# Joined response runs, inputs in twos, and half 0's transfers on POOL's queue, in a fused SSM and feed-forward kernel

## The chip, the cores and the metric

The kernel runs on one core of one Trainium2 chip. A core has a matrix engine (PE, with its weight loads shown apart as PEld), a vector engine (DVE), an activation engine (ACT), a general engine (POOL) and a sequencer that only issues transfers (SP). They run from in-order queues of their own and wait for each other by semaphores. Transfers (DMA) are issued from the queues of SP, ACT or POOL. Matmul results go to PSUM, from which ACT or DVE must copy them before the buffer can be used again. The metric is the time of one execution on the device, in microseconds; lower is better.

## The reference

With `x` of 2048 positions and 576 channels, `xn = layernorm(x)`, the result is `x + S4(xn) + FFN(xn)`:

```python
# S4: a convolution along the 2048 positions, channel by channel
P = exp(dt * A * l)                       # A complex, 576 x 128 states, l = 0..2047
K = einsum("dn,dnl,dn->dl", C, P, dt * B).real
y = irfft(rfft(pad(u)) * rfft(pad(K)))[:2048] + u * Dskip
# FFN
out = silu(x @ w1) @ w2                   # 576 -> 4608 -> 576
```

All inputs and outputs are float32.

## The kernel before, in words

The kernel weaves two programs into one stream per engine. The main one is `ffn()`, the feed-forward part. It goes over two halves of the positions, nine chunks of 512 hidden features and two blocks of 512 positions. `up` multiplies `xn` with `w1` (tile `ph`, lines 314 to 316, three products of high and low parts for float32 accuracy), ACT applies SiLU (`gf`, line 322) and casts to a high part (`gh`, 323), DVE subtracts for the low part (`gl`, 324). `down` multiplies with `w2` (tile `po`, 128 x 288, line 339), and DVE adds the result to the tile `acc` of the positions (343). When half 0 is done, `down` stores each `acc` to memory (`dr0`, 346) and loads the residual input of half 1 into the freed tile (`load_x`, 168).

The other program is `side()`, the convolution, which yields between its steps. `weave` advances it when `ffn` has come to a mark, given as a share of `ffn`'s steps. It has these stages:

- phase 0 normalises the input, transposes it for `up` (the later half through memory, `dxt`, reloaded and split by `next_xt` and `split_xt` at lines 353 to 368), and stores `xn` to `dxn`.
- `kgen()` makes the responses `K` of 288 x 2 channels, 8 x 2 at a time, in 36 steps. DVE and ACT make tables `S` and `C`. After every second step PE multiplies them into `kp` (line 675; the array split into column strips, 128 x 32), ACT copies `kp` to `kt` (682), and PE takes the first transform step from `kt` into two tiles `z` (690; the array split into two row halves, 64 x 128). ACT copies `z` into `stage` (698), and every fourth step SP stores `stage` to `d1k` (703).
- `spread()` gives the inputs the same first step: it loads a tile `xr` of `dxn` (145), splits it into `sp` (ACT 150, DVE 151), multiplies it into `pu` (155, 156), copies it to `u1` (157) and stores it to `d1u` (158). It yields 32 times, two for each `xr`. All its buffers are single.
- `spectral()` has 32 steps, each loading rows of `d1u` and `d1k` (797), splitting them, multiplying (`pk`, `pu`), taking the complex product, multiplying back (`pb`, 805), copying to `yo` (757) and storing to `d2` (758, on POOL's queue).
- `tail()` loads `ys` from `d2` (814), in which every load needs all 32 stores, and `add_conv` multiplies them into `py` (826; the array split into 64 x 32) and adds them to the outputs. The last loads of `w1r` and `w2r` use memory that `spectral` has released.

The tiles `kp`, `z`, `pu`, `pk`, `pb` and `py` share three PSUM buffers (`pss`), `po` three others (`ps2`), `ph` two (`ps1`). The order of instructions on each engine is not written out by hand: a scheduler with its own estimates of durations places each instruction; `tc.high_priority()` puts some ahead, and `behind(ins)` keeps the following ones behind `ins`. So moving a mark or a step moves what stands between others.

The lines of `side()` that set when the stages run:

```python
marks = (0.13, 0.597, 0.823)      # kgen from, spectral from, spectral to
for n, at in enumerate(kgen()):
    if n > 1:
        next(sp, None)
    yield marks[0] + at * (marks[1] - marks[0])
```

Of the kernel before, what the change touches and what calls it, by code (L numbers as in the profile page):

```python
# [11 lines left out]
F32 = mybir.dt.float32  # L12
# [7 lines left out]
P = 128  # L20
# [23 lines left out]
def kernel(  # L44
# [21 lines left out]
    nc = tc.nc  # L66
# [14 lines left out]
    d1k = dram.tile([32 * P, D], F32, name="d1k")  # L81
    d2 = dram.tile([32 * P, D], F32, name="d2")
    dxt = [dram.tile([D, 512], F32, name=f"dxt{b}") for b in range(2)]
    dxn = dram.tile([P, NJ, D], F32, name="dxn")
    dr0 = dram.tile([8 * P, D], F32, name="dr0")
# [26 lines left out]
    acc = {}  # L112
# [23 lines left out]
    def behind(ins):  # L136
        return tc.issue_after(ins) if ins is not None else nullcontext()

    def spread(up):

        s1 = up.tile([P, 2, P], F32R, name="s1", bufs=1)
        nc.gpsimd.dma_start(s1, cs1)
        for j in range(NJ):
            src = up.tile([P, D], F32, tag="xr", name="xr")
            nc.sync.dma_start(src, dxn[:, j])
            for m in range(2):
                lo, hi = slice(64 * m, 64 * m + 64), slice(64 - 64 * m, 128 - 64 * m)
                u1 = up.tile([P, D], F32, tag="u1", name="u1")
                sp = up.tile([P, D], F32R, tag="sp", name="sp")
                nc.scalar.copy(sp[lo, :], src[lo, :])  # L150
                nc.vector.tensor_sub(sp[hi, :], src[lo, :], sp[lo, :])
                for h in range(2):
                    hs = slice(h * HD, (h + 1) * HD)
                    pu = pss.tile([P, 512], F32, tag="pss", name="pu")
                    nc.tensor.matmul(pu[:, :HD], s1[:, 0, :], sp[:, hs], start=True, stop=False)  # L155
                    nc.tensor.matmul(pu[:, :HD], s1[:, 1, :], sp[:, hs], start=False, stop=True)  # L156
                    nc.scalar.copy(u1[:, hs], pu[:, :HD])
                nc.gpsimd.dma_start(
                    d1u.rearrange("(p m j) d -> m j p d", m=2, j=NJ)[m, j], u1)
                yield j  # L160
# [86 lines left out]
    def ffn():  # L247
# [78 lines left out]
        def down(blk, jj):  # L326
            half, c, b = blk
            j = 8 * half + 4 * b + jj
            js = slice(jj * P, (jj + 1) * P)
            if half == 1 and c == NCH - 1:  # L330
                if jj % 2 == 0:
                    add_conv(j, (acc[j], acc[j + 1]))
            for h in range(2):
                hs = slice(h * HD, (h + 1) * HD)
                po = ps2.tile([P, 512], F32, tag="ps2", name="po")
                n = 0
                for t in range(FT):
                    for g, w in ((0, 0), (0, 1), (1, 0)):
                        pins["pe"] = nc.tensor.matmul(po[:, :HD], G[blk, t][g][:, js], W2[half, c, t][w][:, hs],  # L339
                                                      start=n == 0, stop=n == 3 * FT - 1).ins  # L340
                        n += 1
                with tc.high_priority():
                    nc.vector.tensor_add(acc[j][:, hs], po[:, :HD], acc[j][:, hs])  # L343
            if half == 0 and c == NCH - 1:
                rows = slice(j * P, (j + 1) * P)
                nc.sync.dma_start(dr0[rows, :], acc[j])
                if j % 2:
                    acc[7 + j], acc[8 + j] = load_x(7 + j, accp, "acc", (nc.sync,))

        def next_xt(b):  # L350

# [211 lines left out]
    def kgen():  # L563
        fT, phiT = kf["f"], kf["phi"]
        with tc.tile_pool(name="kg", bufs=1) as kg:
# [53 lines left out]
                return th  # L619

            stage = None
            tabs = []
            nxt = head(0)
            al = powers(0)
            for i in range(NCK):
# [52 lines left out]
                                if begins:  # L678
                                    first = mm.ins
                tabs = []  # L680
                kt = kg.tile([P, 512], F32, tag="kt", name="kt")
                nc.scalar.copy(kt, kp)

                z = [pss.tile([P, 512], F32, tag="pss", name="z") for _ in range(2)]
                first = None
                for eg in range(4):
                    for h in (1, 0):
                        rows = slice(64 * h, 64 * h + 64)
                        with tc.high_priority(), behind(first):
                            mm = nc.tensor.matmul(z[h][:, eg * P:(eg + 1) * P], kt[rows, eg * P:(eg + 1) * P], f1[rows],  # L690
                                                  start=True, stop=True, tile_position=(64 * h, 0))
                        first = first or mm.ins
                r = (i - 1) % NRUN
                if r == 0:
                    stage = kg.tile([P, 64, NRUN * CH], F32, tag="stage", name="stage")
                sv = stage[:, :, r * CH:(r + 2) * CH].rearrange("p k (e h c) -> p h e k c", h=2, c=2)
                for h in range(2):
                    nc.scalar.copy(sv[:, h], z[h].rearrange("p (e k c) -> p e k c", e=4, c=2))
                if r == NRUN - 2:
                    d0 = (i // NRUN) * NRUN * CH  # L700
                    kv = d1k.rearrange("(k n) (g d) -> g n k d", n=64, g=2)
                    for gp_ in range(2):
                        nc.sync.dma_start(kv[gp_, :, :, d0:d0 + NRUN * CH], stage[gp_ * 64:(gp_ + 1) * 64])
                yield (i + 1) / NCK

        nc.gpsimd.dma_start(d1k.rearrange("(k n) d -> n k d", n=P)[0],
# [2 lines left out]
    def spectral():  # L709
        def operands(k):  # L710
            rows = slice(k * P, (k + 1) * P)
            return load_part(d1u[rows, :], "u"), load_part(d1k[rows, :], "k")

        def front(k):
            if k % 2 == 0:
                mm = kl.tile([P, 2, 4, P], F32R, tag="mm", name="mm")
                nc.gpsimd.dma_start(mm, cm23[:, k:k + 2])
                mats.append(mm)
            mk = mats[-1][:, k % 2]
            us, ks = ops.pop(k) if k in ops else (split_of(t, n) for t, n in zip(operands(k), "uk"))  # L720
            ka = kl.tile([P, D], F32, tag="ka", name="ka")
            kb = kl.tile([P, D], F32, tag="kb", name="kb", bufs=1)
            y = kl.tile([P, D], F32, tag="y", name="y", bufs=1)
            y2 = kl.tile([P, D], F32, tag="y2", name="y2", bufs=1)
            for h in range(2):
                hs = slice(h * HD, (h + 1) * HD)
                pk = pss.tile([P, 512], F32, tag="pss", name="pk")
                mm3(pk[:, :HD], [(mk[:, 0], mk[:, 1], ks)], hs)
                nc.scalar.copy(ka[:64, hs], pk[:64, :HD])
                nc.scalar.copy(ka[64:, hs], pk[:64, :HD])  # L730
                nc.scalar.mul(kb[:64, hs], pk[64:, :HD], -1.0)
                nc.scalar.copy(kb[64:, hs], pk[64:, :HD])
                pu = pss.tile([P, 512], F32, tag="pss", name="pu2")
                mm3(pu[:, :HD], [(mk[:, 0], mk[:, 1], us)], hs)
                nc.vector.tensor_mul(y[:, hs], pu[:, :HD], ka[:, hs])
                nc.vector.tensor_mul(y2[:64, hs], pu[64:, :HD], kb[:64, hs])
                nc.vector.tensor_mul(y2[64:, hs], pu[:64, :HD], kb[64:, hs])
            nc.vector.tensor_add(y, y, y2)
            return mk, split_of(y, "y")

        mats = []
        first = operands(0)
        yield 1.1
        with behind(pins["gh"]):
            ops = {0: [split_of(t, n) for t, n in zip(first, "uk")]}
        yield 1.12
        nxt = front(0)
        for k in range(32):
            mk, ys = nxt
            if k < 31:  # L750
                nxt = front(k + 1)
            yo = kl.tile([P, D], F32, tag="yo", name="yo")
            for h in range(2):
                hs = slice(h * HD, (h + 1) * HD)
                pb = pss.tile([P, 512], F32, tag="pss", name="pb")
                mm3(pb[:, :HD], [(mk[:, 2], mk[:, 3], ys)], hs)
                nc.scalar.copy(yo[:, hs], pb[:, :HD])
            nc.gpsimd.dma_start(d2.rearrange("(p k) d -> k p d", k=32)[k], yo)
            yield 1 + (k + 1) / 32
# [81 lines left out]

    def side():
        nonlocal s4, kl, yp, pa, tail_at
        marks = (0.13, 0.597, 0.823)
        tail_at = (0.91, 0.934, 0.967, 0.0072)
        with tc.tile_pool(name="kf", bufs=1) as kfp:
            for n in ("f", "phi"):
# [49 lines left out]
            with tc.tile_pool(name="up", bufs=1) as up:  # L897
                sp = spread(up)
                for n, at in enumerate(kgen()):
                    if n > 1:  # L900
                        next(sp, None)
                    yield marks[0] + at * (marks[1] - marks[0])
                for _ in sp:
                    pass
# [97 lines left out]
```

## Time and profile before

| | |
|---|---|
| time of the runs | 1112.2 us, median of 3 (1112.11 to 1112.43) |
| profiled execution | 1112.55 us; span of its instructions 1110.8 us |
| PE busy | 1103.5 us, 99% of the span |
| DVE busy | 917.3 us, 83% |
| ACT busy | 708.0 us, 64% |
| POOL busy | 70.8 us, 6% |
| granted PE clock | 0.999 |

A row of the timeline has the start and the duration in us, the engine, the line of the kernel, the operation, the tiles (written <- read), their sizes and how many records it joins; in brackets the idle time of the engine ahead of it and what ended that. Matmuls overlap, so the distance from one start to the next is their pitch, and the duration is longer than it. A float32 matmul of kp or z shows as two records. A view of one tile or of a window gives the smallest, median and largest duration and the same of the time to a transfer's landing. The view of waits names who waited for whom, the total, how often, and the longest.

### The profile page before, as it was taken

Reading aid. Unit: us, or ns where it says so; the run is one execution under the profiler, and the core shown is the slowest. Engines: PE = TensorE matmul, PEld = TensorE weight load, DVE = VectorE, ACT = ScalarE, POOL = GpSimd, SP = SyncE. Lnnn points to the kernel's source line nnn. Section 1 sums busy time; section 2 is a strip of 40 time slices with the busy share of each in tenths; the row PEclk is TensorE's granted clock in tenths of the full one; section 3 lists DMA queues with packets and bytes.
Section 4 is the critical chain, followed back from the end, with each engine's and each line's share of the span. In section 5 each row is a group of like instructions: output and inputs, shape, how many; then the busy total and the mean of one; then the engine's idle time right before and its main releaser. Section 6 shows DMA issues by size and latency. Waiting matters only on the chain.

```text
span 1110.8 us, 22919 instructions
## 1 busy us (share of the span) xinstructions
PE 1103.5 (99%) x9167; PEld 998.1 (90%) x9167; DVE 917.3 (83%) x1546; ACT 708.0 (64%) x1227; POOL 70.8 (6%) x127
## 2 busy tenths in 40 slices
PE   9999999999999999999999999999999999999998
PEld 6888999899889899899989989999999999999887
DVE  7799899999999999999999837787778778784433
ACT  4574456676777676677866536877777778774210
POOL 1101000000000000011000000000000000000111
PEclk9999999999999999999999999999999999999999
DMA  9745521425242515255834163554544445434973
GB/s 255 204 123 152 140 69 61 120 65 128 82 107 81 133 61 131 76 158 155 217 124 105 44 177 102 168 158 129 161 143 151 140 147 169 131 107 129 255 207 86
DMA packets 175851, 148.56 MB, mean 134 GB/s; under 512 B 111088, under 2 KB 142720, under 8 KB 175616
## 3 DMA queue, kind: packets, MB, share of 16 engines
q1 hardware_dynamic: 165408, 112.69, 38.0%
q0 software_dynamic: 9504, 33.49, 9.4%
q8 instruction: 72, 1.18, 0.5%
q10 hardware_dynamic: 832, 0.92, 0.3%
q14 instruction: 35, 0.29, 0.1%
HBM read 102.53 MB, written 44.61 MB: 132 GB/s over the span
## 4 chain that ended last, share of the span: by engine, by line
PE 94%; DMA 2%; DVE 1%; ACT 1%; SPq 1%; issue 0%; POOL 0%; DVEq 0%; ACTq 0%
PE po L339 40%; PE ph L314 34%; PE kp L675 3%; PE ph L315 3%; PE ph L316 3%; PE pu L805 2%; PE pb L805 2%; PE pk L805 2%; PE z L690 2%; PE pu L155 1%; PE py L826 1%; PE pu L156 1%; DMA acc<-in_A_u_dram 1%; DMA dxn<-xj 1%; DMA w1r<-in_B_w_dram 0%; DMA xj<-in_A_u_dram 0%
## 5 line engine op out<-in xcount | busy, mean ns | idle before, releaser
L339 PE MATMUL po<-w2l,gh 128*128 128x288 f32 x1152 | 339.3, 296 | 0.0
L339 PE MATMUL po<-w2h,gl 128*128 128x288 f32 x1152 | 336.9, 295 | 0.0
L339 PE MATMUL po<-w2h,gh 128*128 128x288 f32 x1152 | 336.1, 296 | 0.0
L339 PEld LDWEIGHTS po<-w2h,gh 128*128 128x128 f32 x1152 | 215.3, 188 | 7.5 <-issue 2.8
L339 PEld LDWEIGHTS po<-w2l,gh 128*128 128x128 f32 x1152 | 216.2, 188 | 5.1 <-issue 0.5
L339 PEld LDWEIGHTS po<-w2h,gl 128*128 128x128 f32 x1152 | 215.7, 188 | 0.8
L322 ACT ACTIVATE gf<-ph 128x512 f32<-128x512 f32 (+1 forms) x148 | 86.3, 584 | 142.8 <-PE ph L316 133.6
L314 PE MATMUL ph<-xh,w1h 128*128 128x512 f32 (+1 forms) x592 | 161.8, 388 | 0.7 <-ACT xh L125 0.6
L314 PE MATMUL ph<-xl,w1h 128*128 128x512 f32 (+1 forms) x592 | 161.7, 386 | 0.2 <-DVE xl L126 0.2
L314 PE MATMUL ph<-xh,w1l 128*128 128x512 f32 (+1 forms) x592 | 161.2, 386 | 0.6 <-DVE w1l L283 0.6
L343 DVE TENSOR_TENSOR acc<-po,acc 128x288 f32<-128x288 f32 x288 | 126.4, 451 | 37.8 <-PE po L339 36.3
L324 DVE TENSOR_TENSOR gl<-gf,gh 128x512 fp32r<-128x512 f32 (+1 forms) x148 | 99.0, 672 | 64.3 <-ACT gh L323 63.5
L314 PEld LDWEIGHTS ph<-xh,w1l 128*128 128x128 f32 x592 | 108.1, 188 | 20.9 <-DVE w1l L283 1.1
L314 PEld LDWEIGHTS ph<-xl,w1h 128*128 128x128 f32 x592 | 108.1, 188 | 20.5 <-DVE xl L126 0.7
L314 PEld LDWEIGHTS ph<-xh,w1h 128*128 128x128 f32 x592 | 104.5, 188 | 17.8 <-ACT xh L125 1.2
L323 ACT CAST gh<-gf 128x512 fp32r<-128x512 f32 (+1 forms) x148 | 89.5, 608 | 10.1 <-PE po L339 7.2
L632 ACT ACTIVATE c<-th,magic 128x1040 f32<-128x1040 f32 x36 | 42.1, 1169 | 37.8 <-DVE C L655 27.9
L634 ACT ACTIVATE c<-th 128x1040 f32<-128x1040 f32 x36 | 38.7, 1075 | 33.9 <-DVE th L633 33.8
L300 ACT CAST w2h<-w2r 128x576 fp32r<-128x576 f32 x72 | 47.0, 671 | 17.3 <-PE po L339 14.9
L283 DVE TENSOR_TENSOR w1l<-w1r,w1h 128x640 fp32r<-128x640 f32 x72 | 57.0, 817 | 0.2
L316 PE MATMUL ph<-x,w1l 128*128 128x512 f32 (+1 forms) x148 | 57.0, 386 | 0.0
L315 PE MATMUL ph<-x,w1h 128*128 128x512 f32 (+1 forms) x148 | 57.0, 385 | 0.0
(182 smaller groups left out, 1830.4 us busy)
## 6 DMA issues: line engine op xcount, KB each, us to landing
w2r<-in_B_w_dram SPq DMA_DIRECT2D x72, 288.0 KB, 3.9
w1r<-in_B_w_dram SPq DMA_DIRECT2D x35, 512.0 KB, 3.7
d1u<-u POOLq DMA_DIRECT2D x32, 288.0 KB, 2.4
d1k<-stage SPq DMA_DIRECT2D x18, 512.0 KB, 6.9
ur<-d1u SPq DMA_DIRECT2D x32, 288.0 KB, 3.9
kr<-d1k SPq DMA_DIRECT2D x32, 288.0 KB, 2.7
d<-yo POOLq DMA_DIRECT2D x32, 288.0 KB, 3.2
ys<-d SPq DMA_DIRECT2D x32, 288.0 KB, 11.3
```

The source lines that it names most:

```text
L283: pins["w1l"] = nc.vector.tensor_sub(l1, src, h1).ins
L300: pins["w2h"] = nc.scalar.copy(h2, r2).ins
L314: nc.tensor.matmul(ph, w[:, kt, :], v[:, kt, a:e], start=n + kt == 0, stop=False)
L315: nc.tensor.matmul(ph, h1[:, 4, :], x4[:, a:e], start=False, stop=False)
L316: pins["pe"] = nc.tensor.matmul(ph, l1[:, 4, :], x4[:, a:e], start=False, stop=True).ins
L322: nc.scalar.activation(gf, ph, AF.Silu)
L323: pins["gh"] = nc.scalar.copy(gh, gf).ins
L324: pins["gl"] = nc.vector.tensor_sub(gl, gf, gh).ins
L339: pins["pe"] = nc.tensor.matmul(po[:, :HD], G[blk, t][g][:, js], W2[half, c, t][w][:, hs], start=n == 0, stop=n == 3 * FT - 1).ins
L343: nc.vector.tensor_add(acc[j][:, hs], po[:, :HD], acc[j][:, hs])
L632: nc.scalar.activation(c65, th, AF.Identity, bias=magic)
L805: nc.tensor.matmul(dst, st, mv[:, hs], start=n == 0, stop=n == 3 * len(terms) - 1)
```

## The change

- In `kgen`, a pair's `z` is no longer issued after its own `kp`, but in the new function `along` after the `kp` of the next pair, behind its last matmul. `kt` gets a second buffer. The last pair's `z` follows its own `kt` as before.
- `spread` is advanced twice after every second step of `kgen`, rather than once after each.
- The load of `xr`, half 0's stores to `dr0` and the residual loads go to POOL's queue rather than SP's.
- The responses' last mark goes from 0.597 to 0.615 of `ffn`'s steps. The first two steps of `spectral` go from 1.1 and 1.12 to 1.06 and 1.08 of its own stretch.

```diff
@@ spread
-            nc.sync.dma_start(src, dxn[:, j])
+            nc.gpsimd.dma_start(src, dxn[:, j])
@@ down
-                nc.sync.dma_start(dr0[rows, :], acc[j])
+                nc.gpsimd.dma_start(dr0[rows, :], acc[j])
                 if j % 2:
-                    acc[7 + j], acc[8 + j] = load_x(7 + j, accp, "acc", (nc.sync,))
+                    acc[7 + j], acc[8 + j] = load_x(7 + j, accp, "acc", (nc.gpsimd,))
@@ kgen
+            kts = []
+            def along(first):
+                nonlocal stage
+                i, kt = kts.pop(0)
+                z = [pss.tile([P, 512], F32, tag="pss", name="z") for _ in range(2)]
+                for eg in range(4):
+                    for h in (1, 0):
+                        rows = slice(64 * h, 64 * h + 64)
+                        with tc.high_priority(), behind(first):
+                            mm = nc.tensor.matmul(z[h][:, eg * P:(eg + 1) * P], kt[rows, eg * P:(eg + 1) * P], f1[rows],
+                                                  start=True, stop=True, tile_position=(64 * h, 0))
+                        first = first or mm.ins
+                ...
                 tabs = []
-                kt = kg.tile([P, 512], F32, tag="kt", name="kt")
+                if kts:
+                    along(mm.ins)
+                kt = kg.tile([P, 512], F32, tag="kt", name="kt", bufs=2)
                 nc.scalar.copy(kt, kp)
-                z = [pss.tile([P, 512], F32, tag="pss", name="z") for _ in range(2)]
-                ...
+                kts.append((i, kt))
+                if i + 1 == NCK:
+                    along(None)
@@ spectral
-        yield 1.1
+        yield 1.06
...
-        yield 1.12
+        yield 1.08
@@ side
-        marks = (0.13, 0.597, 0.823)
+        marks = (0.13, 0.615, 0.823)
...
-                    if n > 1:
+                    if n % 2 == 0 and n:
+                        next(sp, None)
                         next(sp, None)
```

More of the change, by code (lines that the diff above doesn't have):

```diff
@@ L621, in kgen @@
             stage = None
+            kts = []
[10 more added lines that the diff above has]
+                        first = first or mm.ins
+                r = (i - 1) % NRUN
+                if r == 0:
+                    stage = kg.tile([P, 64, NRUN * CH], F32, tag="stage", name="stage")
+                sv = stage[:, :, r * CH:(r + 2) * CH].rearrange("p k (e h c) -> p h e k c", h=2, c=2)
+                for h in range(2):
+                    nc.scalar.copy(sv[:, h], z[h].rearrange("p (e k c) -> p e k c", e=4, c=2))
+                if r == NRUN - 2:
+                    d0 = (i // NRUN) * NRUN * CH
+                    kv = d1k.rearrange("(k n) (g d) -> g n k d", n=64, g=2)
+                    for gp_ in range(2):
+                        nc.sync.dma_start(kv[gp_, :, :, d0:d0 + NRUN * CH], stage[gp_ * 64:(gp_ + 1) * 64])
             tabs = []
@@ L680, in kgen @@
                 tabs = []
-                kt = kg.tile([P, 512], F32, tag="kt", name="kt")
+                if kts:
+                    along(mm.ins)
+                kt = kg.tile([P, 512], F32, tag="kt", name="kt", bufs=2)
                 nc.scalar.copy(kt, kp)
-                z = [pss.tile([P, 512], F32, tag="pss", name="z") for _ in range(2)]
[L685 to L703, printed above, removed]
+                kts.append((i, kt))
+                if i + 1 == NCK:
+                    along(None)
                 yield (i + 1) / NCK
```

## The prediction

> **What bounds the kernel now.** I read the page's head first, then the waits of PE, then PE's timeline around the responses, then the end. The busy line of the page and the waits of PE (who waited for whom: total us, times, longest; five rows in all, first and last shown):
>
> ```profile
> span 1110.8 us, 22919 instructions
> PE 1103.5 (99%) x9167; PEld 998.1 (90%) x9167; DVE 917.3 (83%) x1546; ACT 708.0 (64%) x1227; POOL 70.8 (6%) x127
> ```
>
> ```profile
> PE pz L858 <- DVE zero L853: 1.3, 1, 1.3
> ...
> PE pt L124 <- DVE xn L196: 0.2, 1, 0.2
> ```
>
> PE is busy for all of the span but 7.3 us, and its waits are all in the start-up. So the time is what PE has to do, and only two things can move it: the pace of its stream, and a wait that is not there today. The pace dips where the array's tile shape changes. PE's timeline around one pair of responses (start, us, line, tile, count):
>
> ```profile
> 306.07 0.40 PE L314 MATMUL ph<-xh,w1h 128*128 128x512 f32 x1
> 306.40 0.34 PE L675 MATMUL kp<-C 128*32 128x64 f32 x8
> ...
> 308.15 0.31 PE L675 MATMUL kp<-S 128*32 128x64 f32 x6
> 308.39 0.40 PE L339 MATMUL po<-w2h,gh 128*128 128x288 f32 x1
> 308.64 0.29 PE L339 MATMUL po<-w2l,gh 128*128 128x288 f32 x1
> 308.77 0.30 PE L339 MATMUL po<-w2h,gl 128*128 128x288 f32 x1
> ...
> 312.63 1.07 PE L314 MATMUL ph<-xh,w1h 128*128 128x512 f32 x4
> 313.54 1.07 PE L314 MATMUL ph<-xl,w1h 128*128 128x512 f32 x4
> 314.54 1.16 PE L690 MATMUL z<-f,kt 64*128 64x128 f32 x16
> 315.63 0.40 PE L155 MATMUL pu<-sp,s 128*128 128x288 f32 x1
> 315.87 0.30 PE L156 MATMUL pu<-sp,s 128*128 128x288 f32 x1
> ```
>
> The steady pitch of a 512-column matmul is 0.91/4 = 0.228 us (312.63 to 313.54), of a 288-column one 0.13 (308.64 to 308.77). Against these:
> - The trip into kp costs 0.33 - 0.23 = 0.10 going in. The last kp starts at 308.15 + 0.31 - 0.22 = 308.24 and po 0.15 later, where kp's own pitch is about 0.01: 0.14. The first po then takes 0.25 instead of 0.13: 0.12. Together 0.36.
> - The trip into z costs 1.00 - 0.91 = 0.09 going in. Its 16 records are pairs on the two halves of the array; the last eight, cut out by a narrower window,
>
> ```profile
> 315.08 0.61 PE L690 MATMUL z<-f,kt 64*128 64x128 f32 x8
> ```
>
> start over 0.61 - 0.27 = 0.34 us, three pair pitches of 0.113. Eight pairs are 0.90, but the run lasts 1.09 (314.54 to 315.63): 0.19, about 0.10 at the second pair and 0.09 at the exit. The first pu takes 0.24 instead of 0.13: 0.11. Together 0.39.
>
> **The change part by part.** *Joined runs.* In the order of the changed program's PE instructions 17 of the 18 kp runs are followed at once by the z run of the pair before. No row shows kp next to z. If the passage costs what leaving kp costs (0.14) and z's 0.19 and 0.11 stay, a joined trip costs 0.10 + 0.14 + 0.19 + 0.11 = 0.54 instead of 0.75: 0.21 saved. The ends: 0.12 saved if it pays both an exit and an entry (0.14 + 0.09), 0.45 if it is free and the second pair's 0.10 goes too. I take 0.21, since all four passages seen cost 0.09 or more at the border itself: 17 x 0.21 = **-3.6 us** (ends -2.0 and -7.7).
>
> [...]
>
> *The eighteenth z* stands alone, and the order has split it: four matmuls of one half, 288-column work, then four of the other. That is one more trip (0.39) and no pairing: 16 records at 0.113 instead of eight, 0.9. **+1.3 us.**
>
> *Two additions on SP less, on POOL more.* The xr loads, the stores of half 0 and the residual loads go to POOL:
>
> ```profile
> d1u<-u POOLq DMA_DIRECT2D x32, 288.0 KB, 2.4
> ...
> xr<-dxn SPq DMA_DIRECT2D x16, 288.0 KB, 2.9
> ```
>
> A 288 KB transfer lands in 2.4 us from POOL and 2.9 from SP, so a load is between 0.5 sooner and, behind a store in POOL's order, 2.4 later. An xr now stands directly behind the previous tile's last split; ACT, next in line for it, can wait a little, and ACT is busy 64%: 0 on PE. The first residual load stands 45 us of PE work ahead of its first addition: 0. SP is only relieved, and PE waits for nothing that SP loads: 0.
>
> *The reload of the transposed inputs* moves against its users. In the order after, ACT has between the last ph and the split xh only the SiLU gf, two copies u, one Abs of c and the cast gh. Before:
>
> ```profile
> 494.53 0.77 POOL L353 DMA_DIRECT2D xl<-dxt  x1 [5.04 <-PE ph L314]
> ```
>
> ```profile
> 495.62 0.60 ACT L322 ACTIVATE gf<-ph 128x512 f32<-128x512 f32 x1 [1.92 <-PE ph L316]
> 496.25 0.62 ACT L323 CAST gh<-gf 128x512 fp32r<-128x512 f32 x1
> ...
> 501.90 1.08 ACT L634 ACTIVATE c<-th 128x1040 f32<-128x1040 f32 x1 [1.69 <-DVE th L633]
> ...
> 505.88 1.14 ACT L363 CAST xh<-xl 128x512 fp32r<-128x512 f32 x2
> ...
> 511.05 0.40 ACT L157 COPY u<-pu 128x288 f32<-128x288 f32 x1 [0.20 <-PE pu L156]
> ```
>
> ```profile
> DMA to landing us min/median/max: 8.0/8.0/8.0
> ```
>
> The load lands at 494.5 + 8.0 = 502.5, 6.9 after gf starts, and the split came at 10.3. After, ACT arrives about 3.1 after gf (0.60 + 0.4 + 1.1 + 0.4 + 0.6) and waits 3.8. Behind xh on ACT stands a split sp, on DVE the additions that free po buffers. Three po buffers carry PE about 9 us past gf, nearly enough; the kp run that follows has the slack that a run has today:
>
> ```profile
> 302.83 0.68 DVE L655 SCALAR_TENSOR_TENSOR C<-c,C 128x512 f32<-128x512 f32 x1
> ```
>
> its tables are done at 303.5, 2.9 before the kp at 306.40. So PE loses between 0 and 3.8; I take 3.8 - 2.9, rounded down: **+0.7 us.**
>
> *Responses and inputs in other places.* The same instructions, later marks. The last z ends nearer to the spectral work. Its chain today:
>
> ```profile
> 644.89 1.16 PE L690 MATMUL z<-f,kt 64*128 64x128 f32 x16
> ```
>
> ```profile
> L797 SPq DMA_DIRECT2D kr<-d1k x1: 320/320/320, 660.5 to 660.5; - x1
> ...
> DMA to landing us min/median/max: 5.6/5.6/5.6
> ```
>
> From z's end (646.05) to kr landed (666.1) are 20.0 us. After, ACT comes to that cast 22 us of work behind the last z: covered by 2, cost 0; beyond that ACT would hold a spectral product, not yet PE.
>
> *The end.* The spectral steps move along, and here the cover goes. Timeline rows before (PE, POOL, SP), SP's wait, and the two loads of the second ys tile:
>
> ```profile
> 1012.37 0.29 PE L805 MATMUL pb<-yh,mm 128*128 128x288 f32 x1
> ```
>
> ```profile
> 1013.43 0.54 POOL L758 DMA_DIRECT2D d<-yo  x1 [6.27 <-ACT yo L757]
> ```
>
> ```profile
> SPq L268 <- DMA d<-yo: 10.3, 1, 10.3
> ```
>
> ```profile
> 1019.03 1.29 SPq L814 DMA_DIRECT2D ys<-d  x2
> ...
> 1021.01 2.82 SPq L814 DMA_DIRECT2D ys<-d  x4
> ```
>
> ```profile
> L814 SPq DMA_DIRECT2D ys<-d x2: 637/720/803, 1021.0 to 1021.7; - x2
> ...
> DMA to landing us min/median/max: 11.1/11.3/11.6
> ```
>
> ```profile
> 1034.73 1.23 PE L826 MATMUL py<-ys,s 64*32 64x288 f32 x32
> ```
>
> The last pb must be copied, stored to d, and read back as ys behind five weight loads on SP. The second ys tile lands at 1021.7 + 11.6 = 1033.3, 20.9 us after the last pb; the first py, which needs it, starts 1.4 later. PE fills the stretch with 71 po and 56 ph: 71 x 0.13 + 56 x 0.228 = 22.2, plus 0.2 for pb and the entry, as the rows have it (22.36). In the changed order only 4 po and 69 ph stand between them: 0.5 + 15.7 + 0.2 = 16.4 us. The chain of transfers is the same, in the same order, so PE waits 20.9 - 16.4 = **+4.5 us** at its first py. Ends: the landings of ys over the run are 4.0 to 14.5 us, which makes the wait 0 to 7.4; I take 11.6, the landing of the same load behind the same others. Behind py on PE stand the po of the last chunk, which move along; the next conv products come 10 us of PE work later, and their ys follow in the same queue.
>
> **Sum:** -3.6 + 1.3 + 0.7 + 4.5 = +2.9 us. On the profiled execution (1112.55 us, span 1110.8) that gives 1115.4; the median of the runs is 0.35 lower, 1112.2, so 1115.1 us.
>
> **The rivals.** *The wait at the end does not come*, because ys lands about 5 us sooner (with less in the queue). Then 2.9 - 4.5 = -1.6: 1110.6, not slower. For it: ys lands in as little as 4.0 us elsewhere. Against it: it is the same queue, w1r to ys, and SP sat 10.3 us for the store. It decides once ys needs under 7 us.
>
> *The joined passage is free:* -7.7 instead of -3.6, 1111.0. For it: both tile shapes run beside others of their own shape without a gap. Against: every border between shapes has cost 0.09 to 0.15.
>
> *The second of two inputs is late.* A second pu needs ACT's cast and DVE's subtraction after the first is through:
>
> ```profile
> 291.76 0.29 PE L156 MATMUL pu<-sp,s 128*128 128x288 f32 x1
> ...
> 299.81 0.30 PE L155 MATMUL pu<-sp,s 128*128 128x288 f32 x1
> ```
>
> ```profile
> 297.36 0.75 DVE L151 TENSOR_TENSOR sp<-xr,sp 64x576 fp32r<-64x576 f32 x1
> ```
>
> Here sp is done at 298.1, 6.1 after the pu before it ended (292.05), 1.7 ahead of its user. In the new order six of sixteen gaps are 5.0 to 6.0. At 6.1 they cost 1.1 + 0.7 + 0.5 + 0.4 + 0.1 + 0.1 = 2.9: 1118.0. Against it: the split may also move forward in DVE's order, and it must exceed 5.0 to cost anything.
>
> **Chances.** A measurement of this kernel can tell about 0.2% (2.2 us) from no change: within it lie 1110.0 to 1114.4. The forecast as summed has 0.50; its own range, with a passage from 0.12 to 0.30 saved and a wait of 3.5 to 5.5, is 1112.6 to 1117.7, of which I count 0.40 as slower and 0.10 within. No wait at the end: 0.20, of it 0.12 within and 0.08 faster, where the passage is also cheap. Free passage: 0.12, of it 0.07 within and 0.05 faster. Late second input: 0.18, of it 0.15 slower, and 0.03 divided where another saving meets it (0.01 within, 0.02 faster). Together slower 0.55, within 0.30, faster 0.15. The range from 1109.8 (no wait, and a passage somewhat cheaper than taken) to 1118.8 (late input and a longer ys) leaves out 2 in 10.
>
> **What would show it.** Each kp followed by z with about 0.15 to 0.25 between their starts, and one trip less; the waits of PE with a new row, py on the DMA ys, near 4.5; xh behind a landed xl on ACT by some 3 us; the last z in two runs. The prediction is wrong if py starts at once behind ph, if PE waits for pu or kp in the middle, or if kp to z shows no gap.

## The result and the profile after

The changed kernel takes 1115.67 us (median of 8 runs, 1114.16 to 1116.78), the kernel before 1112.32 us (median of 8 runs beside them). The ratio is 1.0025, with a 95% interval of 1.0015 to 1.0034: 3.3 us slower by the medians, at the edge of what can be told from no change. The profiled execution took 1116.72 us, its span is 1114.9.

First the page's busy line of the kernel after, then PE's waits, all of 0.4 us and more outside the start-up (total us, times, longest):

```profile
span 1114.9 us, 22929 instructions
PE 1104.2 (99%) x9167; PEld 1000.6 (90%) x9167; DVE 917.1 (82%) x1546; ACT 707.3 (63%) x1227; POOL 91.8 (8%) x167
```

```profile
PE py L837 <- DMA ys<-d: 3.2, 1, 3.2
...
PE ph L314 <- ACT gf L322: 1.1, 2, 0.6
...
PE po L339 <- DVE gl L324: 0.4, 1, 0.4
```

Before, PE had no wait behind the start-up. Now there is one of 3.2 us at the first py and a few short ones in the middle. PE's timeline around a joined run (the last kp records, the z, what follows):

```profile
310.47 0.31 PE L702 MATMUL kp<-S 128*32 128x64 f32 x6
310.71 1.16 PE L634 MATMUL z<-f,kt 64*128 64x128 f32 x16
311.80 1.19 PE L314 MATMUL ph<-xh,w1l 128*128 128x512 f32 x4
312.83 0.40 PE L315 MATMUL ph<-x,w1h 128*128 128x512 f32 x1
```

The last kp starts at 310.47 + 0.31 - 0.22 = 310.56 and z 0.15 later; the run of z lasts 1.09, as before; the four ph behind it take 1.03 where 0.91 is usual. And the end, PE's timeline and the loads of the second ys tile:

```profile
1021.30 0.29 PE L816 MATMUL pb<-yh,mm 128*128 128x288 f32 x1
...
1037.40 0.39 PE L316 MATMUL ph<-x,w1l 128*128 128x512 f32 x1
1041.02 2.15 PE L837 MATMUL py<-ys,s 64*32 64x288 f32 x32 [3.23 <-DMA ys<-d]
1043.10 0.61 PE L339 MATMUL po<-w2h,gh 128*128 128x288 f32 x1
1043.50 0.44 PE L339 MATMUL po<-w2l,gh 128*128 128x288 f32 x1
1043.74 0.44 PE L339 MATMUL po<-w2h,gl 128*128 128x288 f32 x1
...
1044.67 0.29 PE L339 MATMUL po<-w2h,gh 128*128 128x288 f32 x1
1044.80 0.30 PE L339 MATMUL po<-w2l,gh 128*128 128x288 f32 x1
```

```profile
L825 SPq DMA_DIRECT2D ys<-d x2: 677/832/987, 1029.9 to 1030.6; - x2
...
DMA to landing us min/median/max: 9.6/9.9/10.2
```

Two things are to be seen here. From the last pb to the landing of ys (1030.6 + 10.2) are 19.5 us, with 16.5 of PE work beside them (1021.30 to 1037.79), and py starts 0.2 after the landing, so PE waits 3.2. And what comes behind the wait is slow: the 32 records of py take 2.08 us instead of 1.16, and po runs at a pitch of 0.24 us instead of 0.13 until 1044.7. The windows of that stretch say why; the column PEclk is the granted clock, 1.00 at full speed:

```profile
1037.00:1041.00 4.00, 0.79 (x4) 0.34 (x3) 2.53 (x4) 1.95 (x4) 0.00 (x0) 1.00 1.08 223
1041.00:1043.00 2.00, 1.98 (x32) 0.98 (x32) 0.00 (x0) 0.00 (x0) 0.00 (x0) 0.55 1.07 271
1043.00:1045.00 2.00, 2.00 (x16) 1.91 (x10) 1.55 (x4) 0.00 (x0) 0.06 (x1) 0.60 1.06 225
1045.00:1050.00 5.00, 5.00 (x40) 5.00 (x39) 1.37 (x3) 0.00 (x0) 1.92 (x4) 1.00 1.09 225
```

PE came back from the wait, and its clock was at one half until 1044.6; the trace's own record of the clock has it at 0.50 from 1041.19 to 1044.61, 3.41 us. PE lost 0.92 us in py and 0.67 in the po behind it: 1.6 us, on top of the 3.2. It was not so in every execution: in two of the eight the mean granted clock was 1.000 and the time 1114.2 and 1114.3 us, in the other six 0.996 to 0.998 and 1114.6 to 1116.8 us, where 3.41 us at half clock lower the mean by 0.0015.

Where the time came from, by the pitches of all PE records in the two traces: the passages of kp and z give 3.4 us back; the eighteenth z, alone and unpaired, takes 1.3; short waits in the middle (at 232.7, 235.0, 349.2 and 564.6 us) take 1.7 (by the distances of starts; as idle time between records, which overlap, it shows as 1.1); the wait at py and the slow stretch behind it take 4.8. That makes +4.4; the profiled executions differ by 1116.72 - 1112.55 = 4.2.

### The profile page after: what moved, and what is told of

It reads as the page before. It is cut to its first block, busy times and chain, and to the rows that moved or that the text cites. A ratio compares the mean times of both kernels' runs of the same rounds, so it can differ in the third digit from the quotient of the medians.

```text
span 1114.9 us, 22929 instructions
## 1 busy us (share of the span) xinstructions
PE 1104.2 (99%) x9167; PEld 1000.6 (90%) x9167; DVE 917.1 (82%) x1546; ACT 707.3 (63%) x1227; POOL 91.8 (8%) x167
## 4 chain that ended last, share of the span: by engine, by line
PE 67%; issue 19%; DVE 4%; DMA 4%; ACT 2%; POOL 2%; SPq 1%; POOLq 0%; DVEq 0%; ACTq 0%
PE po L339 30%; PE ph L314 24%; PE kp L702 3%; PE ph L315 2%; PE ph L316 2%; PE z L634 2%; DMA eb<-dexp 1%; POOL d L769 1%; PE py L837 1%; DMA ys<-d 1%; PE pk L816 1%; PE pu L816 1%; PE pu L155 1%; PE pu L156 1%; DMA acc<-in_A_u_dram 1%
```

## The experiments

Each kernel was timed against the kernel before on the same chip; ratios have 95% intervals, and "idle in the middle" is 490 us less PE's busy time from 170 to 660 us, which is 0.0 in the kernel before and 1.1 in the kernel after.

### The joined runs alone

The kernel before, with the part of the diff in `kgen` and nothing else.

```diff
+                if kts:
+                    along(mm.ins)
+                kt = kg.tile([P, 512], F32, tag="kt", name="kt", bufs=2)
```

> The kernel before with the joined runs alone (the z of a pair directly behind the kp of the next one, kt in two buffers); marks, yields, queues and the single inputs stay as before. Theory: the ledger of pitches in the trace after gives 3.4 us saved in 17 trips (1.44 at the borders into z, about 1.8 at the first po behind a run, the rest at the exit), and the lone eighteenth z costs 0.9 for its missing pairing and 0.4 for its trip. Its order has 22.4 us of PE work between the last pb and the first py, as before, so no wait there: -3.4 + 1.3 = -2.1 us, near 1110.2. Rival: the short stalls in the middle of the trace after (232.7, 235.0 and 564.6 us, 1.7 us in all) come from the joined run, whose three ACT copies stand together; then they show here too and the time is near 1111.9, no change.

Measured: 1119.31 us, ratio 1.006 (1.0046 to 1.0073), 6.6 us slower. Both expected times missed. The passage is as cheap here as in the kernel after (0.15 us from kp to z), and there is no wait at py. But PE idles 5.8 us in the middle. Its waits:

```profile
PE pu L155 <- ACT kt L711: 3.1, 4, 1.1
PE po L339 <- ACT w2h L300: 1.6, 2, 1.1
...
PE ph L314 <- ACT gf L322: 1.1, 2, 0.9
```

The first row shows the place. Around one of these waits, ACT's timeline and then PE's:

```profile
387.94 1.16 ACT L659 ACTIVATE c<-th,magic 128x1040 f32<-128x1040 f32 x1 [1.89 <-DVE th L618]
389.01 0.60 ACT L323 CAST gh<-gf 128x512 fp32r<-128x512 f32 x1
389.52 1.35 ACT L281 CAST w1h<-w1r 128x640 fp32r<-128x640 f32 x2
390.77 1.07 ACT L661 ACTIVATE c<-th 128x1040 f32<-128x1040 f32 x1
391.75 0.56 ACT L711 COPY kt<-kp 128x512 f32<-128x512 f32 x1
```

```profile
387.80 1.16 PE L634 MATMUL z<-f,kt 64*128 64x128 f32 x16
...
392.36 0.40 PE L155 MATMUL pu<-sp,s 128*128 128x288 f32 x1 [1.08 <-ACT kt L711]
```

A joined run holds all three small PSUM tiles, one kp and two z. The next pu needs one of them, and the first to come free is kp's, by the copy kt. ACT had stood idle 1.89 us for DVE, and then had kt behind five other operations. Before, kp's tile was free again when z ran, since z is made from the copy. So joining saves its 3.4 us on the borders and takes away the slack of the buffers. The four waits behind kt are 3.1 of the 5.8 us; why w2h and gf came late was not followed up.

### The later marks alone

```diff
-        yield 1.1
+        yield 1.06
-        yield 1.12
+        yield 1.08
-        marks = (0.13, 0.597, 0.823)
+        marks = (0.13, 0.615, 0.823)
```

> The kernel before with the later marks alone (0.615, and 1.06 and 1.08 inside the spectral work). Theory: the later spectral steps alone make the wait at the first py. 16.5 us of PE work stand between the last pb and the first py, the chain of store and loads took 19.5 us after and 20.9 before, so a wait of 3.0 to 4.5 us, and behind it some 3.5 us at half clock, which costs another 1.8 us: +4.8 to +6.3 us, 1117.1 to 1118.6. Rival: the wait in the trace after comes from the stores and loads on POOL's queue or from the inputs in twos; then there is no wait here and the time stays at 1112.3.

Measured: 1123.99 us, ratio 1.010 (1.0087 to 1.0114). The wait at py is there, 3.0 us, so the marks make it, not the queues or the inputs. But the time is 5 us over the upper end, for a second wait that nothing had announced:

```profile
PE po L339 <- ACT w2h L300: 3.6, 1, 3.6
PE py L826 <- DMA ys<-d: 3.0, 1, 3.0
```

```profile
ACT w2h L300 <- DMA w2r<-in_B_w_dram: 14.5, 8, 6.2
```

That load of w2r, and the same load in the kernel before (time from issue to landing):

```profile
L291 SPq DMA_DIRECT2D w2r<-in_B_w_dram x1: 2854/2854/2854, 493.8 to 493.8; - x1
...
DMA to landing us min/median/max: 10.9/10.9/10.9
```

```profile
DMA to landing us min/median/max: 2.9/2.9/2.9
```

With these marks two stores of d1k stand ahead of this load in SP's queue (488.9 and 489.6, landed 5.7 and 8.7 later), and it lands in 10.9 us instead of 2.9. The reload of the transposed inputs is issued close behind it in both kernels (494.2 here, 494.5 before); in the kernel before, the two stores were issued at 476.4 and 477.1 and had landed 9 us ahead of the load. Windows around the wait, PEclk in the third column from the end:

```profile
501.00:505.30 4.30, 0.79 (x6) 0.55 (x5) 0.00 (x0) 0.64 (x2) 0.00 (x0) 0.84 0.62 161
505.30:507.00 1.70, 1.61 (x7) 1.61 (x8) 0.76 (x1) 1.70 (x5) 0.00 (x0) 0.50 0.02 5
```

So this wait is followed by the same half clock; the pitch of po and ph stays doubled (0.24 us for po instead of 0.13) until 510.7.

### The mark 0.597 in the changed kernel

```diff
-        marks = (0.13, 0.615, 0.823)
+        marks = (0.13, 0.597, 0.823)
```

> The kernel after with the mark 0.615 put back to 0.597, all else as after (joined runs, inputs in twos, POOL's queue, 1.06 and 1.08). Its order has 24.1 us of PE work between the last pb and the first py. Theory: the wait at py (3.2 us) and the half clock behind it (1.8 us) both go: 1115.7 - 5.0 = 1110.7 us, and the granted clock over the end is 1.00. Rival 1: the slow py behind the wait belongs to the loads of ys and not to the idle time; then only 3.2 us go, 1112.5. Rival 2: the loads come as late as before against their users at another place; 1115.7.

Measured: 1114.83 us, ratio 1.002 (1.0011 to 1.0029). At the end the first expectation holds: py waits for nothing and the granted clock is 1.00 from 1010 us on. But only 0.8 us of the expected 5 is won, since PE now idles 3.7 us in the middle, with po waiting 2.2 us for the cast w2h, ph 0.5 each for gf and w1h, and pu 0.5 for stage. With the marks at 0.615 that idle time was 1.1. So in this kernel the later mark buys quiet in the middle and pays at the end.

### All three marks put back

```diff
-        yield 1.06
+        yield 1.1
-        yield 1.08
+        yield 1.12
-        marks = (0.13, 0.615, 0.823)
+        marks = (0.13, 0.597, 0.823)
```

> The kernel after with all three marks put back (0.597, 1.1, 1.12). Its order has 18.3 us of PE work between the last pb and the first py, against a chain of 19.5 to 20.9 us: a wait of 1.2 to 2.6 us at the first py. It tells what the length of the wait does to the clock. Theory: a wait well under 3.2 us does not lower the granted clock, py runs at its usual pitch, and the time is 1110.7 + 1.2 to 2.6 = 1111.9 to 1113.3 us. Rival: any wait of over 1 us halves the clock for some 3.5 us, 1.8 us more: 1113.7 to 1115.1.

Measured: 1117.37 us, ratio 1.0043 (1.0030 to 1.0055). The time missed both ranges, for 4.5 us of idle time in the middle, as in the run before this one. What the run was for came out in the profiled execution: PE waits 1.7 us at py, and the granted clock stays up. In two of the kernel's five executions the mean clock was 0.998, so it may have fallen there; where is not on record.

```profile
1040.00:1042.00 2.00, 1.89 (x37) 1.41 (x38) 1.09 (x3) 1.52 (x3) 0.00 (x0) 1.00 1.05 231
```

### The loads and stores back on SP's queue

```diff
-            nc.gpsimd.dma_start(src, dxn[:, j])
+            nc.sync.dma_start(src, dxn[:, j])
-                nc.gpsimd.dma_start(dr0[rows, :], acc[j])
+                nc.sync.dma_start(dr0[rows, :], acc[j])
-                    acc[7 + j], acc[8 + j] = load_x(7 + j, accp, "acc", (nc.gpsimd,))
+                    acc[7 + j], acc[8 + j] = load_x(7 + j, accp, "acc", (nc.sync,))
```

> The kernel after with the xr loads, the stores of half 0 and the residual loads put back from POOL's queue to SP's; all else as after, and PE's order is the same. The prediction's step: these moves are worth 0 on PE, 1115.7 us. Rival, from the run with the later marks alone: there SP carried these loads, a w2r came late enough for ACT to wait 6.2 us for it at 504.7 us, PE waited 3.6 us for the w2h cast and then ran 5 us at half clock; by this the time is 1115.7 + 3.6 + about 2 = 1121 us, with a row po behind w2h at 3 us or more in PE's waits near 500 us.

Measured: 1118.08 us, ratio 1.0051 (1.0039 to 1.0063), 2.4 us slower than the kernel after and between the two expected times. The rival's place is wrong: there is no wait near 500 us, and the idle time in the middle is 1.1 us, unchanged. At the end py waits 3.8 us instead of 3.2. That is 0.6 of the 2.4; the rest was not found. PE's order is the same in both kernels, and matched matmul by matmul the two profiled executions (1118.08 and 1116.72 us) lie 0.35 us apart ahead of that wait, 0.25 of it from the start-up, and 0.8 at PE's last matmul.

### The inputs singly

```diff
-                    if n % 2 == 0 and n:
-                        next(sp, None)
+                    if n > 1:
                         next(sp, None)
```

> The kernel after with the inputs' transform taken singly again, one input at each step of the responses but the first; all else as after. Theory from the run with joined runs alone: a joined run holds all three of the small PSUM tiles (kp and two z), so a pu that follows it waits for ACT's copy kt, which stands behind other work on ACT; there this cost 3.1 us in four waits. Singly, inputs stand behind joined runs again: rows pu behind kt in PE's waits of 2 to 3 us in all, 1115.7 + 2.5 = 1118.2 us. Rival: the twos do nothing for it, since ACT's load is what decides, and the time stays within 1 us of 1115.7.

Measured: 1116.47 us, ratio 1.0031 (1.0019 to 1.0043), 0.8 us over the kernel after, which the intervals don't separate. The rival holds. No row of PE's waits has pu behind kt, though the inputs come singly and the runs are joined. So it is not the twos that keep pu away from kt here.

### The runs apart

The kernel after, with z behind its own kt as before.

```diff
-                if kts:
-                    along(mm.ins)
-                kts.append((i, kt))
-                if i + 1 == NCK:
-                    along(None)
```

> The kernel after with the z of each pair by itself behind its own kt, as before; marks, twos and queues as after. Theory from the pitches: joining saves 3.4 us and loses 1.3 on the eighteenth z, so 2.1 us more than after, 1117.8 us, if no wait changes. Rival: the waits in the middle of the trace after (1.7 us) come from the joined runs and go, which leaves 1116.1 us.

Measured: 1123.01 us, ratio 1.010 (1.0085 to 1.0115), 5 us over the expectation. PE idles 5.4 us in the middle, 3.1 of it at one place, in PE's waits and in ACT's timeline there:

```profile
PE po L339 <- ACT w2h L300: 3.1, 1, 3.1
```

```profile
572.41 0.67 ACT L300 CAST w2h<-w2r 128x576 fp32r<-128x576 f32 x1 [5.38 <-DMA w2r<-in_B_w_dram]
```

Again a load of w2r is late: SP issued it at 567.3, behind two stores of d1k (558.0 and 559.0, landed 7.5 to 10.2 later) and with residual loads under way, and it landed in 5.0 us. Again the clock is at 0.50 behind the wait, and py waits 3.1 us at the end. Both kernels with runs apart and late marks have this wait; the changed kernel, with its queues back or with single inputs too, has late marks and joined runs and does not have it.

### The first two ys tiles on POOL's queue

```diff
-                nc.sync.dma_start(yss[j][64 * h:64 * h + 64],
+                (nc.gpsimd if j < 2 else nc.sync).dma_start(yss[j][64 * h:64 * h + 64],
```

> The kernel after with the four loads of the first two ys tiles on POOL's queue, where they stand directly behind the last store of d, and no longer behind five weight loads on SP; all else as after. Theory: they are issued some 2.5 us sooner (1025.2 instead of 1027.9 to 1030.6) and share the transfers as before, so they land about 2.5 to 3 us sooner: the wait at py falls from 3.2 us to 0.2 to 0.7, too short to lower the clock, and the time is 1115.7 - 2.5 - 1.8 = 1111.4 us. Rival: the loads land no sooner, as the engines that move them are full in that stretch; 1115.7 us.

Measured: 1111.97 us, ratio 1.000 (0.9991 to 1.0008), 3.7 us under the kernel after. The theory holds. PE's timeline and the last three of the four loads, the last of which is issued at 1027.2 instead of 1030.6:

```profile
1037.90 1.23 PE L837 MATMUL py<-ys,s 64*32 64x288 f32 x32 [0.82 <-PE ph L316]
```

```profile
L825 POOL DMA_DIRECT2D ys<-d x3: 619/624/628, 1025.9 to 1027.2; - x3
...
DMA to landing us min/median/max: 6.9/8.8/10.1
```

ys lands at 1037.3, 3.5 us sooner. The wait is 0.8; py starts 0.6 after the landing, where it was 0.2 in the kernel after, and what held it for the difference was not found. py takes its usual 1.23, and the granted clock is 1.00 from there to PE's end.

### The same, with the eighteenth z in pairs

```diff
-                if i + 1 == NCK:
-                    along(None)
                 yield (i + 1) / NCK
+                if i + 1 == NCK:
+                    yield 1.01
+                    along(pins["pe"])
```

> The kernel after with two edits: the first two ys tiles on POOL's queue, as in the run before this one, and the eighteenth z put 14 us of PE work later, where both its PSUM tiles are free, so that it runs in pairs and in one run; the spectral steps move with it, and 18.2 us of PE work then stand between the last pb and the first py (16.5 without it). Theory: against the run with ys on POOL (1112.0) the pairs give 0.9 us, one trip less 0.4, and the rest of the wait at py (0.8 to 1.0) goes, since the chain there took 16.7 us: 1112.0 - 2.2 = 1109.8 us, under the kernel before. Rival: the later start of the spectral work meets a wait of its own (kr behind the stores of d1k); then 1111 to 1113 us.

Measured: 1116.95 us, ratio 1.0036 (1.0024 to 1.0048). The rival holds in kind, a wait at the start of the spectral work, but the time is 4 us over its range. The eighteenth z is one run of pairs (1.29 us instead of 2.57 for its trips), and two new waits take more than that: pk 1.5 us behind the cast kh at the start of the spectral work, ph 1.6 behind the cast w1h at 1038 us. py still waits 0.7, where it was 0.8. In the profiled executions the kernel is 4.6 us behind the run with ys on POOL's queue alone, 1.1 of it from the start-up, where the two do not differ; what the new waits do not explain was not found.

### DVE relieved

The joined runs alone, with one edit; and the same edit on the kernel of the last experiment.

```diff
-                nc.vector.tensor_sub(sp[hi, :], src[lo, :], sp[lo, :])
+                nc.gpsimd.tensor_sub(sp[hi, :], src[lo, :], sp[lo, :])
```

> The run with joined runs alone (1119.3 us), with one edit: the subtraction that makes the second half of a split input sp (32 of them, 0.75 us each) on POOL instead of on DVE. VectorE is 95 to 99% busy from 170 to 580 us in the kernel before and in the joined one. Theory: the waits in the middle of the joined kernel (7 us: pu behind kt, po behind w2h, ph behind gf) come from DVE having no slack, so that what ACT needs from it comes late and then stands in a bunch; with 24 us less on DVE they fall to 2 us or less: about 1114 us. Rival 1: ACT's own order makes them, 1119 us as before. Rival 2: the subtraction on POOL is slow enough to hold up pu itself; over 1119 us, with rows pu behind POOL sp in PE's waits.

> The kernel after with three edits: the first two ys tiles on POOL's queue, the eighteenth z later and in pairs, and the subtraction of sp on POOL instead of DVE. Theory: as the run with the first two (1109.8 us expected), less the waits in the middle of the kernel after (232.7, 235.0, 349.2 and 564.6 us, 1.7 us in all): 1108.1 us. Rival: POOL's subtraction comes late for pu, or holds up the stores of d1u behind it in POOL's order, and PE waits there: 1111 us or more.

Measured: 1131.91 us, ratio 1.0168 (1.0155 to 1.0181), and 1133.00 us, ratio 1.0171 (1.0149 to 1.0194). The second rival of the first run and the rival of the second hold: POOL's subtraction holds up pu. Both runs fail as tests of the theory, because POOL needs three times as long for the subtraction, 2.35 us where DVE takes 0.75 (groups of the first of the two, count, busy time, mean ns):

```profile
L151 POOL TENSOR_TENSOR sp<-xr,sp 64x576 fp32r<-64x576 f32 x32 | 75.2, 2351 | 22.8 <-ACT sp L150 20.9
...
L155 PE MATMUL pu<-sp,s 128*128 128x288 f32 x64 | 19.6, 315 | 12.2 <-ACT kt L711 6.7 <-POOL sp L151 3.7 <-ACT stage L642 1.8
```

Besides the 3.7 us behind POOL, pu waited 6.7 us behind kt, more than the 3.1 without the edit. Whether DVE's load makes the waits in the middle stays open. What is shown is how full it is in that stretch of the kernel before (window; PE, PEld, DVE, ACT, POOL busy):

```profile
170.00:580.00 410.00, 410.00 (x4320) 369.95 (x4321) 398.69 (x598) 289.19 (x437) 19.36 (x35) 1.00 0.42 113
```

DVE is busy 398.7 of 410 us there, 97%, against 83% over the whole span.

### py a little later

The kernel with ys on POOL's queue, and

```diff
-        tail_at = (0.91, 0.934, 0.967, 0.0072)
+        tail_at = (0.91, 0.936, 0.967, 0.0072)
```

> The run with the first two ys tiles on POOL's queue (1112.0 us), with one edit: the place of the first additions of the convolution is put from 0.934 to 0.936, so that 17.6 us of PE work stand between the last pb and the first py instead of 16.5. The order up to there is the same. Theory: of the wait of 0.8 to 1.0 us that was left at the first py, all but 0.1 goes: 1112.0 - 0.9 = 1111.1 us. Rival: the po that now stand between the ph there wait for something of their own (w2h, gl), or py only waits at the next place; 1112.0 us or more.

Measured: 1112.30 us, ratio 0.9997 (0.9988 to 1.0006). The wait at the first py is gone and nothing is won. PE's waits show a new one of 0.5 us, po behind w2l, as the rival said, and the profiled execution was 0.7 us longer in its start-up (pt behind xn 1.4 us, not 0.7); the rest was not found. No kernel here beat the one before; two equal it, this one and the one with ys on POOL's queue and nothing else.

## Why the prediction was right, and where it was not

The time (1115.7 against 1115.1) and the sign came out as said. The terms of the sum did so only in part.

- *Joined runs, -3.6.* Right: 3.4. Each of the 17 borders from kp to z cost 0.15 us, the value taken, and z's second pair, its exit and the first matmul behind it cost what they did before. So the passage is not free. What the step left out is the buffers: a joined run holds all three small PSUM tiles. Alone, the joining cost 6.6 us, with 3.1 us of waits behind kt; the changed kernel has none of these.
- *The eighteenth z, +1.3.* Right: two runs, 0.9 for the pairs and 0.4 for the trip.
- *Queues, 0.* Wrong: with the transfers back on SP the changed kernel is 2.4 us slower, 0.6 of it in the wait at py, so the moves to POOL were worth something; most of the 2.4 stays open. That PE waits for nothing that SP loads was so in the kernel before; by the prediction's own last step the wait at py is for loads in SP's queue.
- *Reload of the inputs, +0.7.* The wait did not come. The load was issued at 492.4 and landed 6.3 later (8.0 before), at 498.7; ACT came to the first split at 500.25, 1.5 us after that. The order that the step gave directly ahead of the split was right: 2.8 us from gf to xh, where it said 3.1. What it had wrong is which gf to count from. It set the landing against the gf that follows the release of the load (495.62 before, 493.76 after), and ACT's work against the last gf ahead of the split, which is one later (497.49). From the same gf, ACT has 6.5 us and the load 4.9. The load and these ACT rows:

```profile
L353 POOL DMA_DIRECT2D xl<-dxt x1: 773/773/773, 492.4 to 492.4; - x1
...
DMA to landing us min/median/max: 6.3/6.3/6.3
```

```profile
493.76 0.59 ACT L322 ACTIVATE gf<-ph 128x512 f32<-128x512 f32 x1
...
497.49 0.60 ACT L322 ACTIVATE gf<-ph 128x512 f32<-128x512 f32 x1 [0.32 <-PE ph L316]
...
500.25 1.14 ACT L363 CAST xh<-xl 128x512 fp32r<-128x512 f32 x2
```

In its place 1.7 us came from four short waits elsewhere, for which the sum had no term. At the largest, at 564.6 us, gf came late, since in ACT's order it stood behind an operation that had waited 1.65 us for DVE:

```profile
563.86 1.07 ACT L661 ACTIVATE c<-th 128x1040 f32<-128x1040 f32 x1 [1.65 <-DVE th L660]
564.84 0.58 ACT L322 ACTIVATE gf<-ph 128x512 f32<-128x512 f32 x1
```

- *Start of the spectral work, 0.* Right: no wait there.
- *The end, +4.5.* Right in its mechanism, and nearly in its size by luck, since two errors cancel. The wait was 3.2, because the chain from the last pb took 19.5 us instead of 20.9 (the store landed in 2.5 us, the load in 10.2 instead of 11.6). And the prediction counted nothing for PE's clock behind the wait, which was 1.6 (the expectations above put it at 1.8). The run with ys on POOL's queue shows the whole: it gives 3.7 us back with 0.8 of the wait left.
- *Rivals.* No wait at the end: refuted. Free passage: refuted, at 0.15. Late second input: PE's waits have no row for sp. That singly taken inputs cost only 0.8 more says that the twos were neither the harm that the rival feared nor much of a help.

What the sum got wrong in kind is that it added parts that do not add. Joined runs alone: +6.6. Late marks alone: +11.3. Both with the twos and POOL's queue: +3.3. All but the joined runs: +10.7. Each part moves the order of ACT, DVE and SP everywhere, and meets collisions that the others avoid.

## What to carry to other kernels

When PE is busy 99% and its feeder 97% in the same stretch, count for each moved step not only its instructions but which buffers it holds together and which copy frees the first of them. Put a price on a long wait beyond its length: the clock behind it, here 1.6 us behind a wait of 3.2. And run parts alone as well as undone, since here the joined runs alone and the marks alone were each worse than all parts together.

## What the runs showed of the hardware

- There are eight waits of PE of 2.8 to 3.8 us, in six profiled kernels. In or behind seven of them the granted clock fell to 0.50; for the eighth, the 3.6 us with single inputs, the figure is the mean clock of that execution, 0.997. In six it stayed at 0.50 for 3.4 us by the windows; in the kernel after, the trace's record of the clock has 3.413. In the late-marks kernel, behind the wait of 3.6, it stayed for 6.8 us, twice that. After waits of 0.8 us (ys on POOL's queue) and 1.7 us (all marks put back) it stayed at 1.00. In between, the runs settle nothing: the joined kernel with the subtraction on POOL has no wait over 1.9 us; from 300 to 400 us it idled 5.85 us in all at a clock of 1.00, and from 580 to 650 us 2.24 us in all at 0.98.
- In three executions two falls can be compared, and they lie whole multiples of those 3.413 us apart. In the kernel after, the one behind the wait and the one at the program's end came at 1041.2 and 1116.3, 75.1 us apart, 22 times 3.413. With the late marks alone they came, by the windows, at 503.9 and 1050.1, 546.1 us apart, 160 times; with the runs apart at 572.6 and 1050.5, 477.9 us apart, 140 times. In the late-marks kernel the second one came only 1.4 us after work had resumed, behind a wait of 3.0:

```profile
1048.50:1049.50 1.00, 0.84 (x32) 0.65 (x32) 0.00 (x0) 0.00 (x0) 0.00 (x0) 1.00 1.07 230
1049.50:1050.50 1.00, 1.00 (x19) 0.69 (x4) 0.60 (x2) 0.00 (x0) 0.00 (x0) 0.79 1.03 287
1050.50:1051.50 1.00, 1.00 (x6) 1.00 (x6) 0.95 (x3) 0.00 (x0) 0.00 (x0) 0.50 1.07 289
```

- A subtraction of 64 x 576 took 0.75 us on DVE and 2.35 us, by its mean of 32, on POOL.
- A 288 KB load landed in 2.9 us with a reload issued 0.25 us behind it, and in 10.9 us where two stores of its own queue, issued 4 to 5 us ahead of it, were still under way besides.
